# Spectral filter gated by a feed-forward net: the last residue chunk kept in SBUF, output rows requested half a tile sooner, another order at the second chunk's start

## The chip, the cores and the metric

The kernel runs on one core of a Trainium2 chip. The metric is the device time of one execution in microseconds; the time before is the median of three runs. The engines are named as in the profile: PE is TensorE, DVE is VectorE, ACT is ScalarE, POOL is GpSimd, SP is SyncE, whose queue issues most of the DMAs.

## The reference

```
xn  = layernorm(x)                                   # x: 1 x 2048 x 1024
s   = irfft2(rfft2(xn) * (w_r + 1j * w_i))           # over both axes
g   = silu(silu(xn @ w1) @ w2)                       # w1: 1024 x 3584, w2: 3584 x 1024
out = x + s * g
```

All is in float32.

## The kernel before

**Chunks and rows.** The 2048 rows of x are cut into 4 chunks (c) of 4 x 128 rows (p). In every large product the operands are split into a high and a low float16 half, and three passes are summed in PSUM: high by high, high by low and low by high.

**First stage** (0 to about 610 us): per chunk the layer norm, a transposed copy `xnT[c]` in both halves (`hi` and `lo` of `ln_gen` for chunks 0 and 1, DMA transposes in `turned` for chunks 2 and 3), and then `mm1(c, f)`: the product of one chunk with 128 columns of w1, 24 matmuls of 512 columns. A list `order` fixes in which order the pairs (c, f) run: chunk 0 with f = 0 to 3, chunk 1 with f = 0 to 3, and so on. Products are taken depth by depth, so that each needs both halves from the start; the pair (0, 0) alone takes the high-by-high pass first, then high by low, then low by high. `weights1` splits the columns of w1 just ahead of them (line 251 the high half on ACT, line 254 the low half on DVE). The hidden layer is written to DRAM as seven sums for seven products.

**FILL.** At two pairs (c, f) a piece of the spectral transform, `fa_mat` (24 matmuls of 128 columns into a PSUM buffer of the pool `pt`, tag `ft`, two buffers), is put ahead of `mm1`, with `fa_evac`, which copies it out with two ACT instructions (lines 775 and 776). The first is put at the pair (1, 0).

**Second stage**: seven products `(m, j)`, m from 0 to 6 and j from 0 to 7, each tile 42 matmuls of 512 columns in two halves k of 21, whose results are combined to the four blocks of `h @ w2`. Half way through each tile come `settle`, `load_parts` (loads of partial sums pl, line 527), `tick` (deferred stores) and `work` (a slot of background work); at the end of the tile `acc` registers what is to be done with the result, and the same calls follow. A result's evacuation runs half a tile later, its silu (line 615) at that tile's end, and half a tile after that `finish_out`: on DVE the product with the rows of s (line 608) and the sum with the rows of x (line 609), then the output store (line 611). Results become final in the products m = 4, 5 and 6 (`FINALS`). The rows that they need, fs from the residue s (kept in the DRAM tensors sd) and fx from x, are requested by `acc` through `rows_for` (line 548). The last tile (6, 7) is cut into pieces of 256, 128 and 128 columns.

**Background work**: beside both stages run generators for the spectral transform, one slot at a time. A planner with a clock of PE and one of DVE, advanced by fixed costs of each instruction that is written, decides how many slots are emitted between two products. The inverse transform `i_gen(c)` goes over the chunks in the order `IORDER` = 1, 3, 0, 2: it loads the chunk's coefficients (`zt`, one buffer of 16 KB a partition), copies the edge terms into them (line 1166 for an even chunk), multiplies (`mat`, line 1189 or 1181), combines, multiplies again (`mat2`, line 1271), and `bfly(p)` writes the residue's rows s of one block p (lines 1308 to 1315), which are then stored to sd (line 1326). Chunk 1 and 3 are done when m = 4 reaches the tiles that use them, chunk 0 and 2 later.

**Order on the queues.** The program is written in a fixed order, and each engine takes its instructions in that order; SP's DMAs wait in their turn for the buffers and the data that they need. `tile_of` hands out buffers of a tag, and stores that hold a buffer are written before their turn when it runs short.

Of the kernel before, what the change touches and what calls it, by code (L numbers as in the profile page):

```python
# [10 lines left out]
F32 = mybir.dt.float32  # L11
# [12 lines left out]
IORDER = (1, 3, 0, 2)  # L24
SUMMED = (4, 5)
TURNED = (2, 3)
FILL = ((1, 0), (3, 0))
EXTRA = (4, 5, 6, 7, 20, 22, 24)


# [97 lines left out]
def spectral_ffn(ctx, tc, x, w_r, w_i, w1, w2, ca, kc, ci, tw, pm, out):  # L128
    nc = tc.nc
# [45 lines left out]
    def tick():  # L175
        due = []
        for d in deferred:
            d[0] -= 1
            if d[0] <= 0:
                due.append(d)  # L180
        for d in due:
            deferred.remove(d)
            d[1]()
# [19 lines left out]
    def tile_of(pool, shape, dtype, name, tag, bufs):  # L203
        while len(held.get(tag, ())) >= bufs - 1:
            d = held[tag][0]
            deferred.remove(d)
            d[1]()
        return pool.tile(shape, dtype, name=name, tag=tag, bufs=bufs)
# [240 lines left out]
    def mm1(c, f):  # L449
        ps = pf.tile([128, 512], F32, name=f"pa{c}_{f}", tag="ff")  # L450
        w, xt = w1t[f], xnT[c]
        terms = [(d, wh, xh) for wh, xh in ((0, 0), (0, 1), (1, 0)) for d in range(8)]
        if c + f:
            terms.sort(key=lambda k: k[0])
        for n, (d, wh, xh) in enumerate(terms):
            nc.tensor.matmul(ps, w[:, wh, d], xt[:, xh, d], start=(n == 0), stop=(n == 23))  # L456
        if c == 3:
            used1.add(f)
        q, g = f // 2, c // 2

        def evac():
            if (q, g) not in h32:
                h32[q, g] = H["p"].tile([128, 4, 512], F32, name=f"h32_{q}_{g}", tag="h32", bufs=2)
            hq = h32[q, g]
            nc.scalar.activation(hq[:, 2 * (c % 2) + f % 2], ps, AF.Silu, scale=s1[:, f:f + 1])  # L465
            if c % 2 and f % 2:
                return hidden(q, g)

        return evac
# [37 lines left out]

        return second

    stile, queues, fins, sstore = {}, {}, {}, {}  # L510
    part, ht = {}, {}

    def load_h(m, j, k, queue=nc.scalar):
# [7 lines left out]
    rows = {}  # L521
    READS = ((), (), (), (), (1, 0), (), (2, 0))

    def load_parts(m, j):
        for k in READS[m]:
            t_ = tile_of(H["p"], [128, 512], F32, f"pl{m}_{j}_{k}", "pt", 6)
            nc.sync.dma_start(t_, pd[k, j])
            part[k, j] = t_
# [11 lines left out]
    def rows_for(c, p, h, pool, tags):  # L540

        hsl = slice(h * 512, (h + 1) * 512)
        if (c, p) in sstore:
            sstore.pop((c, p))()
        t_ = []
        for name, src, (tag, bufs) in (("fs", sd[c, p], tags[0]), ("fx", xs[4 * c + p], tags[1])):
            t_.append(tile_of(pool, [128, 512], F32, f"{name}{c}_{p}_{h}", tag, bufs))
            nc.sync.dma_start(t_[-1], src[:, hsl])
        return t_

    def acc(m, j, ps, cols=slice(0, 512)):
        tt = nc.vector.tensor_tensor
        g, p = j // 4, j % 4
        tags = (("kept", 8), ("kept", 8)) if m == 6 else (("fs", 3), ("fx", 2))
        for c, h in FINALS[m]:
            if (2 * g + c, p) in stile and (2 * g + c, p, h) not in rows:
                rows[2 * g + c, p, h] = rows_for(2 * g + c, p, h, H["p"], tags)

        def fresh(name):
            return tile_of(H["p"], [128, 512], F32, f"{name}_{j}", "pt", 6)  # L560

        def keep(k, t_):
            store("pt", 3, lambda: nc.sync.dma_start(pd[k, j], t_))

        def evac():
            if m == 0:
                kept[j] = H["p"].tile([128, 512], F32, name=f"kept{j}", tag="kept", bufs=8)
                nc.scalar.activation(kept[j], ps, AF.Copy)
            elif m == 1:
                t_ = fresh("c11")  # L570
                tt(t_, kept[j], ps, op=OP.subtract)
                keep(0, t_)
            elif m == 2:
                tt(kept[j], kept[j], ps, op=OP.add)
            elif m == 3:
                t_ = fresh("c21")
                nc.scalar.activation(t_, ps, AF.Copy)
                tt(kept[j], kept[j], ps, op=OP.subtract)
                keep(1, t_)
            elif m == 4:  # L580
                t_, u = part.pop((1, j)), part.pop((0, j))
                tt(t_, t_, ps, op=OP.add)
                tt(u, u, ps, op=OP.add)
                keep(0, u)
                return final(2 * g + 1, p, 0, t_)
            elif m == 5:
                t_ = fresh("c12")
                nc.scalar.activation(t_, ps, AF.Copy)
                tt(kept[j], kept[j], ps, op=OP.add)
                keep(2, t_)  # L590
                return final(2 * g + 1, p, 1, kept.pop(j))
            else:
                t_, u = part[2, j][:, cols], part[0, j][:, cols]
                tt(t_, t_, ps, op=OP.subtract)  # L594
                tt(u, u, ps, op=OP.add)
                a_, b_ = final(2 * g, p, 1, t_, cols), final(2 * g, p, 0, u, cols)

                def both():
                    x_, y_ = a_(), b_()
                    return (lambda: (x_ and x_(), y_ and y_(), None)[2]) if x_ or y_ else None  # L600

                return both

        return evac
# [534 lines left out]
    def load_i(c):  # L1139
        zt = C["p"].tile([128, 8192], F16, name=f"zt{c}", tag="zt", bufs=1)  # L1140
        if c % 2:
            src = zd[c].rearrange("(m e) q h (r x) -> r m e (q h) x", e=2, r=2)
            dst = zt.rearrange("m (e k x) -> m e k x", e=2, k=8)
            for r in range(2):
                for e in range(2):
                    nc.sync.dma_start(dst[64 * r:64 * r + 64, e], src[r, :, e])
        else:
            nc.sync.dma_start(zt.rearrange("m (q h x) -> m q h x", q=4, h=2), zd[c])
        k = C["p"].tile([128, 2064], F16, name=f"kk{c}", tag="kk", bufs=1)
        nc.sync.dma_start(k, ki[c])  # L1150
        C["z"][c], C["k"][c] = zt, k

    def i_gen(c):
        ip = C["p"]
        tt, stt = nc.vector.tensor_tensor, nc.vector.scalar_tensor_tensor
# [105 lines left out]
            stt(s_[:, 1], u, 2.0**-18, s_[:, 0], op0=OP.mult, op1=OP.subtract)  # L1261
            us[g] = s_

        psd = {}

        def mat2(p):
            ps = pt.tile([128, 4, 256], F32, name=f"id{c}_{p}", tag="ft")
# [8 lines left out]
        def bfly(p):  # L1276
# [14 lines left out]
            pc, qp, u, t_ = pa[:, 0, 0], pa[:, 0, 1], pa[:, 1, 0], pa[:, 1, 1]  # L1291
            pm_, qm, r, v = dm[:, 0, 0], dm[:, 0, 1], dm[:, 1, 0], dm[:, 1, 1]
            o12 = kf[:, 0:256].rearrange("s (n d) -> s n d", n=2)
            s_ = ip.tile([128, 8, 128], F32, name=f"s{c}_{p}", tag="s", bufs=2)
            sides = s_.rearrange("s a (h d) -> s (a h) d", h=2)

            def both(j):
# [17 lines left out]
            stt(both(3), pair(o12[:, 1]), -RH, pair(qp), op0=OP.mult, op1=OP.add)  # L1315
            sf = s_.rearrange("s a b -> s (a b)")
            stile[c, p] = True
            waiting = [h for h in range(2) if (c, p, h) in fins]
            for h in waiting:
                hsl = slice(h * 512, (h + 1) * 512)  # L1320
# [1 line left out]
                nc.sync.dma_start(o, gd[c, p, h])  # L1322
                nc.sync.dma_start(x_, xs[4 * c + p][:, hsl])
                finish_out("fs", c, p, h, o, sf[:, hsl], x_)
            if len(waiting) < 2:
                sstore[c, p] = lambda: nc.sync.dma_start(sd[c, p], sf)
                defer(1, lambda: (c, p) in sstore and sstore.pop((c, p))())

# [7 lines left out]
            yield 3.9 if 2 <= i <= 4 else 2  # L1336
        if c != IORDER[-1]:
            load_i(IORDER[IORDER.index(c) + 1])
        yield PAUSE
        for p in range(5):  # L1340
            if p < 4:
# [45 lines left out]
    with tc.manual_schedule():  # L1387
# [134 lines left out]
        for n, (m, j) in enumerate(seq):  # L1522
            if 0 < n < len(seq) - 2:
                for k in range(n == 1, 2):
                    load_h(*seq[n + 2], k, nc.scalar)
            if n == len(seq) - 1:
                load_parts(m, j)
                for b, cols in enumerate((slice(0, 256), slice(256, 384), slice(384, 512))):
                    ps = pf.tile([128, cols.stop - cols.start], F32, name=f"pb{m}_{j}_{b}", tag="ff")
                    for k in range(2):  # L1530
                        mm2(m, j, ps, k, cols)
                    for _ in range(4):
                        settle()
                        tick()
                    after(acc(m, j, ps, cols))
                break
            ps = pf.tile([128, 512], F32, name=f"pb{m}_{j}", tag="ff")
            for k in range(2):
                while ready2[0] < m * NP + 7 * k + 6:
                    slot(wq)  # L1540
                mm2(m, j, ps, k)
                if k == 0:
                    settle()
                    load_parts(m, j)
                    tick()
                    work()
            if j == 7:
                done2[0] = m + 1
            after(acc(m, j, ps))
            if m == 0:  # L1550
                slot(wq)
# [38 lines left out]
```

## Time and profile before

| what | value |
|---|---|
| median of three runs | 1242.93 us (1242.85 to 1243.19) |
| the profiled execution | 1243.2 us |
| its span, first to last instruction | 1241.3 us |
| PE busy | 1221.6 us, 98% |
| DVE busy | 999.3 us, 80% |
| ACT busy | 468.2 us, 38% |
| POOL busy | 116.0 us, 9% |
| DMA | 297.87 MB, mean 240 GB/s |

A busy PE is not PE at its peak, since matmuls are pipelined. Idle time of an engine that isn't the bottleneck costs nothing; what counts is where PE, or the stretch behind its last matmul, waits. A line of the timeline has start and duration in us, the engine, the line of the kernel, the operation, what is written from what, and in brackets the idle time ahead of it and what ended it.

### The profile page before, as it was taken

The page shows a single profiled execution, that of the slowest core. Times are in us where ns is not written, and L with a number is a line of the kernel's source. Part 1 is how long each engine was busy: PE and PEld are TensorE (multiplying, and loading weights), DVE is VectorE, ACT ScalarE, POOL GpSimd, SP SyncE. Part 2 cuts the span into 40 slices and gives each one's busy share as a digit, 9 for nine tenths or more (in the row PEclk, how much of TensorE's full clock was granted, in tenths as well). Part 3 has the DMA queues.
Part 4 walks back from the last instruction along what each step waited for, and adds up shares of the span by engine and source line. Part 5 has one row for each costly group of instructions (what it writes and reads, how often), then busy time and mean ns, then how long its engine had stood idle before and what let it go on. Part 6 is the DMA issues. An engine that isn't in the chain of part 4 may idle for free.

```text
span 1241.3 us, 19106 instructions
## 1 busy us (share of the span) xinstructions
PE 1221.6 (98%) x7033; PEld 625.4 (50%) x7033; DVE 999.3 (80%) x1974; ACT 468.2 (38%) x614; POOL 116.0 (9%) x241
## 2 busy tenths in 40 slices
PE   8999999999999999999999999999999999899997
PEld 5545445444544454445445555544545555455554
DVE  7687988899798898887969899794297588796886
ACT  4865344334554555435433222122132232242212
POOL 2230000001000000010001121114111110000000
PEclk9999999999999999999999999999999999999999
DMA  7487486646668897759899999997989989887797
GB/s 254 134 172 182 134 231 203 187 140 175 204 189 243 279 275 235 221 183 270 189 293 250 282 260 206 270 261 224 293 214 283 285 286 342 311 326 267 269 334 247
DMA packets 272831, 297.87 MB, mean 240 GB/s; under 512 B 40289, under 2 KB 199009, under 8 KB 272353
## 3 DMA queue, kind: packets, MB, share of 16 engines
q1 hardware_dynamic: 252720, 237.85, 66.1%
q10 hardware_dynamic: 15984, 51.45, 11.9%
q0 software_dynamic: 4032, 7.34, 3.4%
q8 instruction: 55, 0.90, 0.3%
q14 instruction: 40, 0.32, 0.1%
HBM read 188.05 MB, written 104.35 MB: 236 GB/s over the span
## 4 chain that ended last, share of the span: by engine, by line
PE 71%; DVE 13%; DMA 10%; issue 3%; ACT 2%; SPq 1%; POOL 0%; ACTq 0%; DVEq 0%; POOLq 0%
PE pa L456 45%; PE pb L536 7%; PE pb L535 7%; PE pb L534 7%; DVE Z L1039 2%; DMA fx<-in_A_x_dram 2%; PE id L1271 1%; DMA zd<-zq 1%; DMA wq<-in_A_w_i_dram 1%; DVE w L254 1%; DVE T L1004 1%; DMA pl<-pd 1%; DMA zt<-zd 1%; DMA ht<-hd_sum_d 1%; DVE zq L970 1%
## 5 line engine op out<-in xcount | busy, mean ns | idle before, releaser
L456 PE MATMUL pa<-xnT,w 128*128 128x512 f16 x2688 | 585.2, 379 | 1.1 <-ACT w L251 0.7
L456 PEld LDWEIGHTS <-w 128*128 128x128 f16 x2688 | 262.1, 98 | 311.7 <-DVE w L254 1.3
L534 PE MATMUL pb<-w,ht 128*128 128x512 f16 (+2 forms) x812 | 300.4, 372 | 0.0
L535 PE MATMUL pb<-w,ht 128*128 128x512 f16 (+2 forms) x812 | 300.4, 372 | 0.0
L536 PE MATMUL pb<-w,ht 128*128 128x512 f16 (+2 forms) x812 | 300.3, 372 | 0.0
L536 PEld LDWEIGHTS <-ht 128*128 128x128 f16 x812 | 79.4, 98 | 91.0
L534 PEld LDWEIGHTS <-ht 128*128 128x128 f16 x812 | 79.5, 98 | 86.9
L535 PEld LDWEIGHTS <-ht 128*128 128x128 f16 x812 | 79.5, 98 | 86.9
L465 ACT ACTIVATE h<-pa,s 128x512 f32<-128x512 f32 x112 | 75.6, 679 | 121.9 <-PE pa L456 109.8
L251 ACT ACTIVATE w<-jr,sc 128x512 f16<-128x512 f32 x98 | 68.2, 713 | 80.9 <-PE pb L536 25.4
L254 DVE SCALAR_TENSOR_TENSOR hoone<-h,hs,hoone 128x2048 f16<-128x2048 f32 x28 | 65.7, 2346 | 8.4 <-ACT hoone L251 8.4
L254 DVE SCALAR_TENSOR_TENSOR w<-jr,sc,w 128x512 f16<-128x512 f32 x98 | 71.1, 744 | 1.2 <-ACT w L251 1.2
L251 ACT ACTIVATE hoone<-h,hs 128x2048 f16<-128x2048 f32 x28 | 56.0, 1998 | 37.5 <-DVE h L499 24.6
L251 ACT ACTIVATE hosum<-hr,hs 128x1536 f16<-128x1536 f32 x28 | 44.1, 1574 | 64.8 <-DVE hr L495 31.2
L965 ACT ACTIVATE zq<-Z,zs 128x1024 f16<-128x1024 f32 x16 | 18.4, 1148 | 104.8 <-DVE Z L1039 57.8
L254 DVE SCALAR_TENSOR_TENSOR hosum<-hr,hs,hosum 128x1536 f16<-128x1536 f32 x28 | 50.7, 1812 | 3.4 <-ACT hosum L251 3.4
L494 DVE TENSOR_TENSOR hr<-h 128x1024 f32<-128x1024 f32 x28 | 34.2, 1222 | 23.9 <-ACT h L465 23.8
L251 ACT ACTIVATE w<-w1r,rs 128x1024 f16<-128x1024 f32 x28 | 32.0, 1144 | 47.0 <-DVE w L254 31.8
L274 DVE TENSOR_REDUCE m<-w1r 128x1 f32<-128x1024 f32 x28 | 33.8, 1211 | 16.5 <-DMA w1r<-in_B_w_dram 16.5
L615 ACT ACTIVATE pl<-pl,c 128x512 f32<-128x512 f32 (+2 forms) x28 | 17.4, 656 | 76.3 <-DVE pl L594 44.5
L938 PE MATMUL fx<-vq,kq 128*128 128x256 f16 x192 | 43.2, 272 | 0.0
L939 PE MATMUL fx<-vq,kq 128*128 128x128 f16 x192 | 42.0, 219 | 0.0
(210 smaller groups left out, 1524.5 us busy)
## 6 DMA issues: line engine op xcount, KB each, us to landing
w1r<-in_B_w_dram SPq DMA_DIRECT2D x28, 512.0 KB, 6.3
hd_sum<-hosum SPq DMA_DIRECT2D x56, 256.0 KB, 2.9
hd_one<-hoone SPq DMA_DIRECT2D x56, 256.0 KB, 3.6
hd_dif<-hoone SPq DMA_DIRECT2D x56, 256.0 KB, 3.2
w2m<-in_B_w_dram SPq DMA_DIRECT2D x28, 512.0 KB, 5.2
ht<-hd_dif ACTq DMA_DIRECT2D x32, 448.0 KB, 6.2
jr<-in_B_w_dram SPq DMA_DIRECT2D x56, 256.0 KB, 6.4
ht<-hd_sum ACTq DMA_DIRECT2D x32, 448.0 KB, 6.6
```

Of the source, the lines that this page charges most:

```text
L251: nc.scalar.activation(hi, raw, AF.Copy, scale=scale)
L254: nc.vector.scalar_tensor_tensor(lo, raw, scale, hi, op0=OP.mult, op1=OP.subtract)
L274: nc.vector.tensor_reduce(m1[:, i:i + 1], raw[i], axis=AX.XY, op=OP.max, apply_absolute_value=True)
L456: nc.tensor.matmul(ps, w[:, wh, d], xt[:, xh, d], start=(n == 0), stop=(n == 23))
L465: nc.scalar.activation(hq[:, 2 * (c % 2) + f % 2], ps, AF.Silu, scale=s1[:, f:f + 1])
L494: tt(sums[:, 0:2], hq[:, 0::2], hq[:, 1::2], op=OP.subtract)
L534: nc.tensor.matmul(ps, hh[:, 0], w[:, 0], start=first, stop=False)
L535: nc.tensor.matmul(ps, hh[:, 0], w[:, 1], start=False, stop=False)
L536: nc.tensor.matmul(ps, hh[:, 1], w[:, 0], start=False, stop=last)
L938: nc.tensor.matmul(o, k[:, c, kh, 1], v[:, c, vh], start=(n == 0), stop=False)
L939: nc.tensor.matmul(ps[:, c, 0], k[:, c, kh, 2], v[:, c, vh, 128:256], start=False, stop=False)
L1039: eng.tensor_tensor(Z[:, ns, pos], x0[:, :, ls], x1[:, :, ls], op=o_)
```

## The change

Three things are changed.

1. The first fill moves from the pair (1, 0) to the pair (1, 1), and `mm1(1, 0)` takes its high-by-high pass first, as (0, 0) does.
2. A function `ahead_rows`, taken out of `acc`, requests the rows for a tile's final results half way through that tile, right behind `load_parts`; in the last tile it is called ahead of the three pieces. `acc` still calls it for rows that weren't there yet.
3. The rows s of the chunk that is transformed last, chunk 2, are written into one tile of 4 blocks that takes the buffer of `zt`. They aren't stored to sd, and `rows_for` hands out views of that tile in place of loads.

```diff
-FILL = ((1, 0), (3, 0))
+FILL = ((1, 1), (3, 0))
...
     def mm1(c, f):
...
-        if c + f:
+        if f or c > 1:
             terms.sort(key=lambda k: k[0])
...
     def rows_for(c, p, h, pool, tags):
...
         for name, src, (tag, bufs) in (("fs", sd[c, p], tags[0]), ("fx", xs[4 * c + p], tags[1])):
+            if name == "fs" and (c, p) in resident:
+                t_.append(resident[c, p][:, hsl])
+                continue
             t_.append(tile_of(pool, [128, 512], F32, f"{name}{c}_{p}_{h}", tag, bufs))
             nc.sync.dma_start(t_[-1], src[:, hsl])
...
-    def acc(m, j, ps, cols=slice(0, 512)):
-        tt = nc.vector.tensor_tensor
+    def ahead_rows(m, j):
         g, p = j // 4, j % 4
         tags = (("kept", 8), ("kept", 8)) if m == 6 else (("fs", 3), ("fx", 2))
         for c, h in FINALS[m]:
             if (2 * g + c, p) in stile and (2 * g + c, p, h) not in rows:
                 rows[2 * g + c, p, h] = rows_for(2 * g + c, p, h, H["p"], tags)
+
+    def acc(m, j, ps, cols=slice(0, 512)):
+        tt = nc.vector.tensor_tensor
+        g, p = j // 4, j % 4
+        ahead_rows(m, j)
...
         def bfly(p):
...
-            s_ = ip.tile([128, 8, 128], F32, name=f"s{c}_{p}", tag="s", bufs=2)
+            if c == IORDER[-1]:
+                s_ = last_rows[0][:, p]
+            else:
+                s_ = ip.tile([128, 8, 128], F32, name=f"s{c}_{p}", tag="s", bufs=2)
...
             stile[c, p] = True
+            if c == IORDER[-1]:
+                resident[c, p] = sf
...
-            if len(waiting) < 2:
+            if len(waiting) < 2 and c != IORDER[-1]:
                 sstore[c, p] = lambda: nc.sync.dma_start(sd[c, p], sf)
...
         if c != IORDER[-1]:
             load_i(IORDER[IORDER.index(c) + 1])
+        else:
+            last_rows.append(ip.tile([128, 4, 8, 128], F32, name="rows", tag="zt", bufs=1))
...
             if n == len(seq) - 1:
                 load_parts(m, j)
+                ahead_rows(m, j)
...
                 if k == 0:
                     settle()
                     load_parts(m, j)
+                    ahead_rows(m, j)
                     tick()
                     work()
```

More of the change, by code (lines that the diff above doesn't have):

```diff
@@ L508, in hidden @@
         return second
-    stile, queues, fins, sstore = {}, {}, {}, {}
+    stile, queues, fins, sstore, resident = {}, {}, {}, {}, {}
     part, ht = {}, {}
@@ L1262, in split @@
             us[g] = s_
-        psd = {}
+        psd, last_rows = {}, []
         def mat2(p):
```

## The prediction

> **What bounds the kernel now.** I read the page first, then every wait of TensorE (PE) in the span, then the three places where those waits lie, engine by engine.
>
> ```profile
> span 1241.3 us, 19106 instructions
> ```
>
> ```profile
> PE iu L1189 <- DVE zt L1166: 2.8, 1, 2.8
> ...
> PE pa L456 <- DVE w L254: 0.4, 1, 0.4
> ```
>
> The first fence is the page's head, the second the view of waits for PE alone (us in total, times, longest). TensorE waits in very few places, and the change touches three of them: the start, where the second chunk's first product is prepared; the 2.8 us before the third chunk's inverse transform; and the stretch after PE's last matmul, which no wait of PE shows. The windows view below has one short and one long stretch (length, then PE, PEld, DVE, ACT, POOL busy with counts, granted clock, DMA share, GB/s).
>
> ```profile
> 49.36:63.10 13.74, 13.74 (x67) 6.39 (x66) 7.33 (x17) 13.61 (x10) 4.31 (x12) 1.00 0.75 144
> 70.00:840.00 770.00, 770.00 (x4230) 382.74 (x4229) 666.53 (x1248) 322.56 (x381) 63.29 (x115) 1.00 0.79 221
> ```
>
> From 70 to 840 us PE is busy for 770.00 of 770 us: what is lost or won before 70 us is kept to the end, one for one. From 49.36 to 63.10 us ScalarE (ACT) is busy for 13.61 of 13.74 us: anything put into its queue there delays everything behind it. These two rows decide the first part.
>
> **Part 1: the fill and the order of the second chunk's first product.** The timelines of PE, ACT and VectorE (DVE), columns start, duration, instruction, and in brackets the idle time before it and who ended it:
>
> ```profile
> 41.97 1.95 PE L702 MATMUL tp<-ident,x 128*128 128x128 f32 x16
> 45.40 0.22 PE L766 MATMUL fa<-cas,xnT 128*128 128x128 f16 x1 [1.47 <-DVE xnT L710]
> ...
> 46.73 10.52 PE L456 MATMUL pa<-xnT,w 128*128 128x512 f16 x48
> ...
> 68.61 1.69 PE L456 MATMUL pa<-xnT,w 128*128 128x512 f16 x7 [0.42 <-DVE w L254]
> ```
>
> ```profile
> 43.06 1.94 ACT L706 ACTIVATE xnT<-tp 128x1024 f16<-128x1024 f32 x2 [3.09 <-PE tp L702]
> ...
> 46.94 0.61 ACT L775 ACTIVATE L<-fa 128x520 f32<-128x520 f32 x1 [1.36 <-PE fa L768]
> 47.44 0.59 ACT L776 ACTIVATE L<-fa 128x504 f32<-128x504 f32 x1
> 47.91 0.69 ACT L465 ACTIVATE h<-pa,s 128x512 f32<-128x512 f32 x1
> ```
>
> ```profile
> 44.12 2.36 DVE L710 TENSOR_TENSOR xnT<-tp,xnT 128x1024 f16<-128x1024 f32 x2 [2.12 <-ACT xnT L706]
> ...
> 63.26 1.23 DVE L494 TENSOR_TENSOR hr<-h 128x1024 f32<-128x1024 f32 x1 [4.95 <-ACT h L465]
> ...
> 67.27 1.28 DVE L254 SCALAR_TENSOR_TENSOR w<-w1r,rs,w 128x1024 f16<-128x1024 f32 x1
> ```
>
> Before, PE waits 1.47 us for a PSUM buffer, runs the 24 fill matmuls (45.40 to 46.73, so 1.33 us) and then product (1,0) from 46.73. After, (1,0) comes first and its eight high-by-high matmuls need only the high halves, which ACT finishes at 43.06 + 1.94 = 45.00. A matmul takes 10.52/48 = 0.219 us here, so those eight run to about 46.8; the low halves are there at 44.12 + 2.36 = 46.48, so the next pass doesn't wait. PE then runs (1,0) for 24 x 0.219 = 5.25 us and the fill: it gets through about 0.35 us sooner (45.05 against 45.40).
>
> But the two copies of the fill's result (L775, L776) move too. Before, they stand in ACT's queue at 46.94 and take 47.91 - 46.94 = 0.97 us, in a stretch where ACT waits anyway. After, they are written into the program ahead of (1,1) and so behind the normalisation steps that the first background slot after (1,0) emits: inside the stretch from 49.36 to 63.10 that has no room. That slot is emitted either way: the planner's clock of PE is one fill lower there, which isn't enough to hold it back by its constants. So everything that ACT does behind them comes 0.97 us later, with the evacuation h for which DVE waited 4.95 us at 63.26, and behind this in DVE's order the low half of the next weights (L254, done at 67.27 + 1.28 = 68.55), for which PE waited 0.42 us at 68.61. I therefore expect PE at 69.58 instead of 68.61, its wait growing to 0.42 + 0.35 + 0.97 = 1.74 us: **+0.97 us**. If ACT's delay is hidden after all, this part gives -0.35; these are its ends. I take the upper one, since the row of ACT's stretch leaves 0.13 us free.
>
> **Part 2: rows asked for half a tile sooner (fifth to seventh product).** Three timelines' rows around the 2.8 us wait: SP's queue, DVE, and how long the residue's stores (L1326) take to land (min/median/max).
>
> ```profile
> 1050.36 0.44 SPq L548 DMA_DIRECT2D fs<-sd  x1
> 1050.85 0.42 SPq L548 DMA_DIRECT2D fx<-in_A_x_dram  x1
> ...
> 1053.34 0.90 SPq L527 DMA_DIRECT2D pl<-pd  x2
> ```
>
> ```profile
> 1056.84 0.75 DVE L608 SCALAR_TENSOR_TENSOR pl<-fs,s_sc,pl 128x512 f32<-128x512 f32 x1 [1.78 <-DMA fs<-sd]
> 1059.27 0.69 DVE L609 TENSOR_TENSOR pl<-pl,fx 128x512 f32<-128x512 f32 x1 [1.67 <-DMA fx<-in_A_x_dram]
> 1060.65 0.69 DVE L582 TENSOR_TENSOR pl<-pl,pb 128x512 f32<-128x512 f32 x1 [0.69 <-DMA pl<-pd]
> ```
>
> ```profile
> DMA to landing us min/median/max: 3.5/5.6/9.6
> ```
>
> PE's 2.8 us end with the copy at L1166, which stands in DVE's queue right behind these. DVE waits 1.78 us for fs, 1.67 for fx and 0.69 for the partial sums pl. Asked for half a tile sooner, fs and fx are there, so 3.45 us of waiting go; but what is late next is pl, which is asked for at 1053.34 whatever fs does and was waited for last. Only what pl itself moves up counts. The two requests in front of it (0.44 + 0.42 us of SP's time) have then been issued a round earlier, so I take 0.86, say **-0.9 us**. The ends: -2.8 if pl comes so much sooner that the whole wait goes; and a loss, because the moved request sits behind the store it reads. For the chunk whose residue is being made at that time, a row's load must wait for its own store, and before it stood behind four other transfers, now it stands ahead of them: the store of the partial sum, the store of the output, the weights jr and the next pl all queue on SP behind that wait. A store lands after 5.6 us in the median; the half tile gained is about as long, so what is held up is of the order of 0 to 3 us: +3.0 is my upper end. On the issue of a load behind the store that it reads, the Trainium skill's page "DMA: Bandwidth & Descriptors", section "Two DMAs through the same engine are not ordered", says that the same queue gives no order and that the issuing engine has to wait for the first transfer's semaphore. By that page's fixed 2.0 us plus bytes over 436 GB/s, a 512 KB store would cost 3.2 us, my estimate; the row's median of 5.6 is longer and is what I go by.
>
> In the seventh product the second tile's four loads share eight buffers with a result of the sixth product whose output store is written behind them. One of the loads has to wait for that store; behind it on SP stand only a partial sum's store and the next tile's loads, needed more than a tile later: nothing.
>
> **Part 3: the last chunk's rows stay in SBUF.** Four stores of 512 KB and eight loads of 256 KB go. The room is that of the chunk's transform input, which PE has read before the first row is written; no wait is added. Until the last tile this all lies beside PE. Then:
>
> ```profile
> 1220.82 0.95 SPq L527 DMA_DIRECT2D pl<-pd  x2
> ```
>
> ```profile
> 1229.40 4.72 DMA fx<-in_A_x_dram
> ```
>
> ```profile
> 1232.23 0.48 DVE L608 SCALAR_TENSOR_TENSOR pl<-fs,s_sc,pl 128x256 f32<-128x256 f32 x1 [3.69 <-DMA fs<-sd]
> 1232.90 0.43 DVE L609 TENSOR_TENSOR pl<-pl,fx 128x256 f32<-128x256 f32 x1 [0.19 <-DMA fx<-in_A_x_dram]
> 1233.57 0.48 DVE L608 SCALAR_TENSOR_TENSOR pl<-fs,s_sc,pl 128x256 f32<-128x256 f32 x1 [0.24 <-DMA fs<-sd]
> 1234.21 0.42 DVE L609 TENSOR_TENSOR pl<-pl,fx 128x256 f32<-128x256 f32 x1 [0.16 <-DMA fx<-in_A_x_dram]
> ...
> 1236.48 0.28 DVE L594 TENSOR_TENSOR pl<-pl,pb 128x128 f32<-128x128 f32 x1
> ```
>
> ```profile
> 1232.22 0.22 PE L536 MATMUL pb<-w,ht 128*128 128x128 f16 x1
> ```
>
> PE's last matmul ends at 1232.22 + 0.22 = 1232.44, but DVE takes up its result only at 1236.48, since the first of the last tile's three pieces waited 3.69 + 0.19 + 0.24 + 0.16 = 4.28 us for rows (the piece of the chain of waits: a load issued at 1229.40, 4.72 us). After, fs is no transfer, and the two fx loads are issued right behind pl, at about 1221.8 and 1222.3: with 4.72 us each they land by 1227, before DVE wants them at 1232.23 - 3.69 = 1228.54. Without the 4.28 us DVE would reach the last piece at 1232.20, so PE's end is what is late next: about 1232.5. From there to the span's end nothing changes (1241.3 - 1236.48 = 4.82 us). That is **-3.98 us**; a few tenths of activation in front of the first piece are covered by PE's end. The ends are -4.04 and, if the loads don't get ahead, about -1.0 (below).
>
> **The sum**, against the profiled execution's own 1243.2 us (span 1241.3 and 1.9 around it): 0.97 - 0.9 - 3.98 = -3.91, so 1239.3; the median of the three runs, 1242.93, lies 0.27 lower, which gives 1239.0 us.
>
> **The rivals.**
> - *The start gains.* ACT's delay is swallowed and part 1 gives -0.35: 1.32 us less, 1237.7. Against it: the row of ACT's stretch and the 4.95 us for which DVE waits on it.
> - *The middle doesn't gain.* The moved requests hold up about as much as they bring: part 2 between 0 and +3.0, so 1239.9 to 1242.9. For it: pl is the last wait, and it isn't moved.
> - *The tail's loads don't get ahead*, so the change doesn't do there what it says: SP keeps the two fx behind the waiting output stores, and only the two fs issues go, moving the last load from 1229.40 to about 1228.4. Tail -1.0 instead of -3.98: 1242.0. Against it: the call stands in the program directly behind pl's.
> - *Slower: the store-to-load wait on SP.* In tiles 4 to 7 of the fifth product a request goes out right behind a store that takes the longest landing of the row, 9.6 us, and pl, queued behind it, comes 9.6 us later; PE's wait before the third chunk's transform grows from 2.8 to 12.4 us: 1243.2 + 0.97 + 9.6 - 3.98 - 0.27 = 1249.5. It turns the sign beyond the resolution once the hold-up exceeds 2.5 + 3.98 - 0.97 = 5.5 us. For it: TensorE's longest wait hangs on exactly this queue. Against: most landings are near 5.6 us, and the request is made half a tile before its use. The Trainium skill, "TensorE: Matmul & The Clock Gate", section "HAM oscillation — how this bites in real kernels", adds that PE gaps above about 3.4 us bring the clock down; by it this case would cost a little more, and no wait so long stands inside this trace.
>
> **How the numbers follow.** A measurement of this kernel tells 0.2%, about 2.5 us, from no change: faster means below 1240.4, slower above 1245.4. The forecast gets 0.45 and the start's gain 0.15, both faster. The middle gets 0.22, of which 0.08 lies below 1240.4 and 0.14 within. The tail's rival gets 0.10, within; the slower one 0.08. That is faster 0.68, same 0.24, slower 0.08. The range goes from 1236.5 (the start's gain with somewhat more in the middle) to 1243.0 (the middle's upper end); it leaves out the slower case and the rare sum of all gains (-0.35 - 2.8 - 4.04, so 1235.7).
>
> **What would show it.** In the profile after: PE's wait for the fill gone and its wait on the weights' low half at about 1.7 us near 69 us; a wait of about 1.9 us instead of 2.8 before the third chunk's transform, with DVE waiting on pl and hardly on fs or fx; no wait of L608 in the last tile, its last piece taken up within 0.2 us of PE's last matmul, and some 4.8 us from there to the end. I am wrong in part 1 if ACT's copies of the fill delay no h, in part 2 if SP's loads behind the stores grow PE's wait, and in part 3 if the last piece still starts 2 us or more after PE ends.

## The result: slower by two parts in a thousand, and the profile after

| | before | after |
|---|---|---|
| median of 22 executions each (lowest to highest) | 1242.51 us (1239.79 to 1246.35) | 1244.91 us (1240.88 to 1249.37) |
| ratio after / before, 95% interval | | 1.0022 [1.0012, 1.0032] |
| profiled execution, its span | 1243.2 us, 1241.3 us | 1245.52 us, 1243.7 us |
| TensorE's last matmul ends, and from there to the span's end | 1232.44, 8.90 us | 1239.04, 4.66 us |

In the two profiles the change takes 4.2 us off the tail and puts 6.5 us into the middle. Lines stand further down in the kernel after (L548 of before is L551, L608 is L615, L1166 is L1173, L1326 is L1338). The longest wait of PE in the kernel after (us in total, times, longest):

```profile
PE iu L1196 <- DVE zt L1173: 7.5, 1, 7.5
```

Before, this wait was 2.8 us: it is the middle. I go through the three places, start, middle and tail, in order.

**The start came out as written.** PE, ACT and DVE in the kernel after:

```profile
44.94 5.34 PE L456 MATMUL pa<-xnT,w 128*128 128x512 f16 x24 [1.13 <-ACT xnT L713]
...
69.47 3.84 PE L456 MATMUL pa<-xnT,w 128*128 128x512 f16 x17 [1.74 <-DVE w L254]
```

```profile
55.60 0.59 ACT L782 ACTIVATE L<-fa 128x520 f32<-128x520 f32 x1
```

```profile
64.12 1.23 DVE L494 TENSOR_TENSOR hr<-h 128x1024 f32<-128x1024 f32 x1 [6.26 <-ACT h L465]
```

The product starts at 44.94 without waiting for the low halves, the two copies now stand from 55.60 on, inside ACT's full stretch, DVE gets its h 0.86 us later (64.12 against 63.26), and PE waits 1.74 us where it waited 0.42.

**The middle went the other way.** PE, then DVE in the kernel after:

```profile
1066.97 6.91 PE L1196 MATMUL iu<-kk,zt 128*128 128x129 f16 x72 [7.51 <-DVE zt L1173]
```

```profile
1058.91 0.75 DVE L615 SCALAR_TENSOR_TENSOR pl<-fs,s_sc,pl 128x512 f32<-128x512 f32 x1
...
1063.92 0.69 DVE L589 TENSOR_TENSOR pl<-pl,pb 128x512 f32<-128x512 f32 x1 [3.54 <-DMA pl<-pd]
1066.11 0.69 DVE L590 TENSOR_TENSOR pl<-pl,pb 128x512 f32<-128x512 f32 x1 [1.50 <-DMA pl<-pd]
```

DVE waits no more for fs or fx, and pl is the last wait, both as expected. But pl is asked for at 1059.73 instead of 1053.34. SP's queue in the kernel after, and then the same place before:

```profile
1028.24 0.32 SPq L1338 DMA_DIRECT2D sd<-s  x1
1039.84 0.32 SPq L551 DMA_DIRECT2D fs<-sd  x1
...
1040.69 0.46 SPq L570 DMA_DIRECT2D pd<-pl  x1
...
1059.73 2.47 SPq L527 DMA_DIRECT2D pl<-pd  x2
```

```profile
1033.35 0.32 SPq L563 DMA_DIRECT2D pd<-pl  x1
1033.77 0.38 SPq L1326 DMA_DIRECT2D sd<-s  x1
...
1038.66 0.32 SPq L548 DMA_DIRECT2D fs<-sd  x1
```

After, SP issues the store of the first of these residue tiles at 1028.24, and its next instruction, the load of the same rows, goes out at 1039.84: for 11.3 us SP issues nothing. Before, the store went out 5.5 us later (1033.77) and the load 1.2 us sooner (1038.66). So asking half a tile sooner moved the store up but not the load, and the store of the partial sum (pd), which stood ahead of both at 1033.35, came behind them, at 1040.69. The view of SP's waits splits the 11.3 us between two landings (us in total, times, longest): 5.1 us for the transform input zt, then 6.1 for the store.

```profile
SPq L551 <- DMA sd<-s: 7.4, 2, 6.1
...
SPq L551 <- DMA zt<-zd: 5.1, 1, 5.1
```

The chain of waits shows what slides behind (start, us, what):

```profile
1028.24 11.58 DMA sd<-s
...
1042.23 8.62 DMA sd<-s
...
1052.81 9.05 DMA out_dram<-pl
1061.88 4.21 DMA pl<-pd
```

The store took 11.58 us to land, the second 8.62, and the output store that went out late behind them holds the buffer into which the second pl is loaded. The landing of all residue stores was 3.5/5.6/9.6 us (min/median/max) before; after:

```profile
DMA to landing us min/median/max: 4.7/8.2/12.8
```

A second loss stands in PE's row: the 72 matmuls take 6.91 us. The windows view, first after, then before (length, then PE, PEld, DVE, ACT, POOL busy with counts, granted clock, DMA share, GB/s):

```profile
1062.00:1067.00 5.00, 0.03 (x1) 0.03 (x2) 1.49 (x3) 1.33 (x2) 0.00 (x0) 0.53 0.95 267
1067.00:1075.00 8.00, 8.00 (x78) 7.30 (x79) 4.13 (x10) 1.15 (x4) 0.00 (x0) 0.65 0.82 290
```

```profile
1062.00:1067.00 5.00, 4.20 (x71) 4.03 (x71) 2.62 (x5) 1.89 (x5) 0.00 (x0) 1.00 1.03 381
```

The granted clock is 0.53 in the second part of the long gap and 0.65 behind it. Before, with a gap of 2.8 us, it stays at 1.00, and PE's next product starts 5.00 us after the first of the same matmuls (1067.11 - 1062.11, a wait of 0.70 included) instead of 6.74 (1073.71 - 1066.97).

**The tail came out as written.** SP and DVE in the kernel after:

```profile
1226.85 0.95 SPq L527 DMA_DIRECT2D pl<-pd  x2
1227.85 0.91 SPq L551 DMA_DIRECT2D fx<-in_A_x_dram  x2
```

```profile
1235.39 0.48 DVE L615 SCALAR_TENSOR_TENSOR pl<-rows,s_sc,pl 128x256 f32<-128x256 f32 x1 [0.25 <-ACT pl L622]
...
1239.08 0.29 DVE L601 TENSOR_TENSOR pl<-pl,pb 128x128 f32<-128x128 f32 x1
```

No DMA stands in a bracket of these pieces any more, and DVE takes up the last one at 1239.08, 0.04 us after PE's end.

**The sum by places.** Each number is how much later than in the profile of before the same matmul of the products starts (the same place in PE's order), at about 73 us, at 1020 us (the middle not yet begun) and behind the third chunk's first transform product (1067.11 us before). The last two columns are from PE's end to the span's end, and the span.

| kernel (experiments below) | 73 us | 1020 us | 1067 us | middle: 1067 less 1020 | tail | span |
|---|---|---|---|---|---|---|
| before | 0 | 0 | 0 | 0 | 8.90 | 1241.34 |
| after | +0.86 | +0.15 | +6.60 | +6.45 | 4.66 | 1243.70 |
| e1_no_ahead_4_7 | +0.85 | +3.22 | +2.23 | -0.99 | 4.66 | 1239.34 |
| e2_other_rows | +0.88 | +0.73 | +0.44 | -0.29 | 4.66 | 1237.54 |
| e3_only_4_7 | -0.14 | +3.38 | +6.10 | +2.72 | 9.66 | 1248.20 |
| e4_tail_only | -0.33 | -1.03 | -2.11 | -1.08 | 4.65 | 1234.98 |
| e5_filled_gap | +0.70 | -0.01 | +4.06 | +4.07 | 4.65 | 1241.15 |
| e6_start_only | +0.82 | +0.80 | -0.29 | -1.09 | 9.25 | 1241.40 |
| e7_calm_tiles | -0.28 | +3.07 | +2.38 | -0.69 | 4.65 | 1239.46 |
| e8_fx_early | +1.27 | +5.13 | +4.60 | -0.53 | 4.66 | 1241.70 |
| e9_store_act | +1.29 | +1.45 | +6.31 | +4.86 | 4.65 | 1243.40 |
| e10_resident_only | -0.12 | +4.56 | +3.10 | -1.46 | 7.63 | 1243.17 |
| e11_ask_only | -0.05 | -0.72 | -2.25 | -1.53 | 6.29 | 1236.48 |
| e12_both | -0.26 | -0.97 | -2.78 | -1.81 | 4.65 | 1234.32 |

For after: 0.15 + 6.45 - 4.24 = +2.36, the difference of the spans. From 1067 us to PE's end no kernel moves by more than 0.01 us. The column at 1020 us needs care: e3, e4, e10, e11 and e12 issue up to there what before issues, and yet they stand between -1.03 and +4.56 us there (why, stands in the last section). So one profile's span says little at this size; the columns "middle" and "tail" and the ratios over many executions do. The other kernels without early requests in tiles 4 to 7 of the fifth product (e8's for x aside) have a middle of -0.7 to -1.8, so the profile of before was itself on the long side there by some 1 us. A tail that nothing changes took 8.90, 9.25 and 9.66 us (before, e6, e3).

### The profile page after: what moved, and what is told of

Same layout as the page of the kernel before. It is cut to its first block, busy times and chain, and to the rows that moved or that the text cites. A ratio compares the mean times of both kernels' runs of the same rounds, so it can differ in the third digit from the quotient of the medians.

```text
span 1243.7 us, 19101 instructions
## 1 busy us (share of the span) xinstructions
PE 1222.9 (98%) x7033; PEld 627.7 (50%) x7033; DVE 999.3 (80%) x1974; ACT 467.6 (38%) x614; POOL 115.8 (9%) x241
## 4 chain that ended last, share of the span: by engine, by line
PE 88%; DMA 5%; DVE 4%; ACT 2%; issue 1%; SPq 0%; POOL 0%; ACTq 0%; DVEq 0%; POOLq 0%
PE pa L456 45%; PE pb L536 12%; PE pb L534 12%; PE pb L535 12%; PE fx L945 2%; DMA sd<-s 2%; PE id L1278 1%; DMA out_dram<-pl 1%; PE iu L1196 1%; PE fx L947 1%; PE fx L946 1%; DMA jr<-in_B_w_dram 1%; ACT xp L700 1%; PE fa L773 1%; PE iu L1188 1%
```

## The experiments

Each kernel ran beside the kernel before on the same chip, and its ratio is to those executions; three chips were used (e1 to e4, e5 to e8, e9 to e12), so medians in us are compared within one of these groups only. Each median is of 12 executions (e3: 6), and each profile is of one.

Theory: part 2 costs, because in tiles 4 to 7 of the fifth product a load now stands directly behind the store of the rows it reads, SP waits there until the store has landed, and pl is queued behind it. Rivals: the start costs more than its 1 us; any early request costs through fuller DMA engines; the resident rows cost something.

### Take the early requests out of those four tiles

```
                     load_parts(m, j)
-                    ahead_rows(m, j)
+                    if m != 4 or j < 4:
+                        ahead_rows(m, j)
```

> The kernel after, but in tiles 4 to 7 of the fifth product (m = 4) the rows are requested at the tile's end as before. Theory (the hold): there SP stands at a load that must wait for the store it reads, and pl is asked for late; without it PE's wait before the third chunk's transform (7.5 us after, 2.8 before) falls to 4 us or less, the granted clock stays at 1.00 in that stretch, and the time is 3 to 5 us below the kernel before (tail -4.2, start +0.15). Rival (elsewhere): the early requests of the other tiles or the missing stores move the queue; then the wait stays at 6 us or more and the time is 1 to 3 us above the kernel before.

Measured: median 1240.26 us, ratio to before 0.9981 [0.9966, 0.9995].

```profile
PE iu L1196 <- DVE zt L1173: 1.8, 1, 1.8
```

```profile
1062.00:1070.00 8.00, 5.48 (x79) 4.46 (x78) 4.85 (x11) 2.26 (x5) 0.00 (x0) 1.00 1.04 385
```

With four requests moved back, the wait is 1.8 us, the clock 1.00, and the kernel is faster than before. The middle is 7.44 us shorter than in the kernel after: its loss is in these four tiles. The time fell by less than expected, 2.0 us below before (1242.28 here) instead of 3 to 5; in the trace 3.22 us arose ahead of 1020 us.

### Keep the early requests, but read rows that are already stored

The load of fs takes rows of the second chunk, stored long ago, in place of the fourth's (so these rows of the output are wrong).

```
+        src_c = 1 if c == 3 and h == 0 else c
-        for name, src, (tag, bufs) in (("fs", sd[c, p], tags[0]), ...
+        for name, src, (tag, bufs) in (("fs", sd[src_c, p], tags[0]), ...
```

> The kernel after with the same order, count and size of transfers, but in tiles 4 to 7 of the fifth product fs is read from the residue of the second chunk, stored long before, in place of the fourth chunk's just stored (so these output rows carry the wrong residue). Theory (the hold): no load waits for a store, PE's wait falls to 3 us or less and the time is 3 to 5 us below the kernel before. Rival (order and bandwidth): two transfers of 256 KB stand ahead of what DVE needs whether they wait or not; then PE's wait stays at 6 to 8 us and the time is 1 to 3 us above the kernel before.

Measured: median 1242.03 us, ratio 0.999 [0.9976, 1.0004]. SP's queue, then PE's wait:

```profile
1028.63 0.32 SPq L1339 DMA_DIRECT2D sd<-s  x1
1034.86 0.32 SPq L552 DMA_DIRECT2D fs<-sd  x1
```

```profile
PE iu L1197 <- DVE zt L1174: 2.5, 1, 2.5
```

Same instructions, same order, same bytes; only the load no longer reads what the store writes. SP waits 5.9 us (for the landing of the transform input, not of the store) instead of 11.3, PE 2.5 us instead of 7.5. So it is the wait for the store's landing, not the traffic; of the 11.3 us, 5.9 would have passed without it. The expected time, 3 to 5 us below before, was missed: the interval of the ratio reaches from -3.0 to +0.5 us. Against the kernel after, the ratios differ by 0.0032, 4.0 us, which is less than the trace's 6.7 (6.45 + 0.29).

### Only those four tiles' requests, on the kernel before

```
+                    if m == 4 and j >= 4:
+                        ahead_rows(m, j)
```

> The kernel before with the early request in tiles 4 to 7 of the fifth product alone. Theory (the hold): this alone makes PE wait 6 to 8 us, the clock falls behind the wait, and with no gain in the tail the time is 5 to 7 us above the kernel before. Rival (order and bandwidth): two transfers of some 0.65 us each, 0 to 1.5 us above the kernel before.

Measured: median 1250.26 us, ratio 1.0057 [1.0039, 1.0076], so +7.1 us. PE's wait and the windows:

```profile
PE iu L1193 <- DVE zt L1170: 4.3, 1, 4.3
```

```profile
1062.00:1070.00 8.00, 3.71 (x34) 3.12 (x32) 1.49 (x3) 1.48 (x3) 0.00 (x0) 0.79 0.95 298
```

Four requests alone make the kernel clearly slower, and the price agrees with the difference of the ratios of after (1.0022) and the tail alone (0.9964), 0.0058. But in its one profile PE's wait is only 4.3 us, where 6 to 8 were expected, and the middle +2.72; 3.38 of its span arose ahead of the first of these requests and 0.76 in the tail. How much of the 7.1 us in six executions is the four requests' own is therefore open. A gap of 4.3 us too is followed by a clock below 1.00.

### Only the tail part

The kernel after with the start undone and without `ahead_rows` in mid tile (the last tile's call stays).

> The kernel before with the last chunk's rows in SBUF and the early request in the last tile alone (start and all other tiles as before). Theory: the tail's -4.2 us are all here and the middle is untouched: PE's wait 2 to 4 us, time 3.5 to 5 us below the kernel before. Rival (the tail needs the early requests of the tiles ahead of it): a gain of 1 to 3 us.

Measured: median 1237.39 us (1235.32 to 1242.6), ratio 0.9964 [0.9948, 0.998]; tail 4.65 us. This version beats both kernels. It ran again on another chip, beside its two halves, as e12_both below.

### Fill the gap in front of the transform

In the kernel after, 50 matmuls on idle data go ahead of the transform's first product, into the same PSUM tile.

```
             psu[g] = ps
+            if c == 0 and g == 0:
+                for _ in range(50):
+                    nc.tensor.matmul(ps[:, 0:256], idle[:, 0:128], idle, start=True, stop=True)
```

> The changed kernel, with 50 idle matmuls of 256 columns (about 5.4 us) put on TensorE ahead of the third chunk's first transform product, into a gap of 7.5 us there. Theory: the granted clock of 0.52 to 0.80 after that gap is made by the gap itself. Then the 72 matmuls after it take about 5.2 us as before instead of 6.9, the clock in 1062 to 1075 us stays at 0.95 or more, and the time is 1.7 us below the changed kernel's: about 1243.2, ratio to before 1.0006. Rival: the clock falls there for another reason (the power state of that moment, as it does in 845 to 855 us in some runs): the 72 matmuls still take 6.5 us or more and the time stays at 1244.9. In both the wait for the last row and its transfer stay as long as they were.

Measured: median 1244.74 us, ratio 1.0014 [1.0001, 1.0027]. PE, then the windows:

```profile
1059.13 5.62 PE L1184 MATMUL iu<-ones 128*128 128x256 f16 x50
1066.17 2.92 PE L1201 MATMUL iu<-kk,zt 128*128 128x129 f16 x48 [1.42 <-DVE zt L1173]
```

```profile
1062.00:1067.00 5.00, 3.58 (x41) 3.06 (x39) 1.49 (x3) 1.33 (x2) 0.00 (x0) 1.00 0.89 251
1067.00:1075.00 8.00, 7.30 (x79) 5.05 (x77) 5.31 (x12) 2.46 (x5) 0.00 (x0) 1.00 0.79 299
```

The data still comes late (1066.17), but the clock stays at 1.00 and from there to the next product it takes 5.00 us (1071.17 - 1066.17) instead of 6.74. So the gap makes the clock fall, and that costs 1.74 us of the 6.45. The times can't tell: the median lies near the rival's 1244.9 us, but before ran 0.65 us longer here than in the first table, and the ratio's interval holds the theory's 1.0006 as well as 1.0022.

### Only the start

> The kernel before with only the first part of the change: the filler moved to the second column block and the second chunk's first product sorted high-by-high pass first. Theory: TensorE stands 0.8 to 1.0 us later at 73 us, and 0.1 to 0.9 us later from 850 us on, since a wait for the edge product there takes part of it back; 1242.5 to 1243.4, ratio 1.0001 to 1.0008. Rival: the start is worth 3 us at the end (the difference of the kernel without requests in tiles 4 to 7 and the one with only the tail part, 1240.3 against 1237.4): 1245.

Measured: median 1242.88 us, ratio 0.9998 [0.9985, 1.0011]. PE:

```profile
69.43 2.76 PE L456 MATMUL pa<-xnT,w 128*128 128x512 f16 x12 [1.74 <-DVE w L254]
```

The wait is there to the hundredth and PE is 0.82 us late at 73 us, but over 12 executions nothing can be measured: the interval reaches from -1.9 to +1.4 us. The rival of 3 us is out.

### Early requests everywhere but in the four tiles, start as before

> The kernel with only the tail part, and rows asked for half a tile sooner in all tiles but 4 to 7 of the fifth product, that is, wherever no store of the same rows is pending. Theory: without a store to wait for, the early requests change nothing that TensorE waits for: 1236.9 to 1237.9, within 0.5 us of the kernel with only the tail part (1237.4), TensorE's wait for the third chunk's transform input at 1.5 to 2.8 us. Rival: early requests cost wherever they stand, through the DMA queues: 1239 to 1240.

Measured: median 1240.74 us, ratio 0.9973 [0.9958, 0.9988], against 0.9964 [0.9948, 0.998] with the tail alone on another chip. PE's wait is 2.1 us, the middle -0.69, and 3.07 us of its span came up ahead of 1020 us. The median missed the expected 1236.9 to 1237.9. On this chip before ran 0.9 us longer too; with that taken off, it lies in the rival's range (1239 to 1240), and the two ratios can't be told apart. What speaks against the rival is the trace, where neither the wait nor the middle shows a cost. A gain of these requests isn't seen either.

### Ask early for x alone in the four tiles

```
+                    else:
+                        early[c, p, 0] = tile_of(H["p"], [128, 512], F32, f"fx{c}_{p}_0", "fx", 2)
+                        nc.sync.dma_start(early[c, p, 0], xs[4 * c + p][:, 0:512])
```

> The changed kernel, but in tiles 4 to 7 of the fifth product only the rows of x are asked for in mid tile; the rows of the residue, and with them their store, come at the end of the tile as before. Theory: it is the wait of the residue rows' load for their store's landing that holds the queue: without it pl of tile 4 is asked for by 1054 us and TensorE waits 1.7 to 2.8 us; about 1240.3, as without any early request there. Rival: any 256 KB more in that stretch pushes pl back: the wait is 4 to 6 us and the time 1242 to 1243.5.

Measured: median 1242.06 us, ratio 0.9985 [0.997, 1.0].

```profile
PE iu L1201 <- DVE zt L1178: 2.3, 1, 2.3
```

In the trace an early load in the same place does no harm if it reads nothing that is being stored: the wait is within the theory's 1.7 to 2.8, not the rival's 4 to 6, and the middle is -0.53. The ratio is near that of e1 (0.9981), but the median lies in the rival's range (1242 to 1243.5). pl was asked for at 1058.30 in its trace, but PE itself stood 5.13 us later there, so the 1054 of the expectation isn't a fair mark.

### Issue the store on another queue

```
-                sstore[c, p] = lambda: nc.sync.dma_start(sd[c, p], sf)
+                sstore[c, p] = lambda: nc.scalar.dma_start(sd[c, p], sf)
```

> The changed kernel, with the stores of the residue's rows issued on ScalarE's DMA queue instead of SyncE's. Theory: the store took 11.6 us to land because it stood behind a 2 MB load in its own queue; on the other queue it lands within 6 us, SyncE is held at most 5 us, pl of tile 4 is asked for by 1056 us and TensorE waits 2 to 4 us there; about 1241, ratio 0.998 to 1.0. Rival: it lands late because all queues share the same 16 DMA engines: it still takes 9 us or more, the wait stays at 6 us or more, and the time at 1.001 to 1.003.

Measured: median 1245.59 us, ratio 1.0009 [0.9993, 1.0025]. The chain of waits and PE's wait:

```profile
1027.24 11.61 DMA sd<-s
```

```profile
PE iu L1196 <- DVE zt L1173: 6.0, 1, 6.0
```

My theory here was wrong. The store doesn't land late because it stands behind the 2 MB transform input in SP's queue: on ScalarE's queue it takes 11.61 us, as on SP's (11.58). The view of DMAs counts all queues against the same 16 engines, and those are full: 1026 to 1042 us of the kernel after in 40 slices, busy tenths and GB/s:

```profile
DMA  9989799999989697999999999999974209576999
GB/s 384 503 321 530 291 506 387 454 442 378 408 336 555 253 518 324 405 302 294 284 286 291 261 354 389 400 430 420 410 312 184 102 20 87 102 128 113 224 347 319
```

They work through a backlog until about 1038 us, and move little around 1039.84, when the held load at last goes out: SP has issued nothing in the meantime. That the backlog, and not a place in a queue, makes the store late is my reading: ScalarE's queue too had two loads ahead of the store, issued at 1020.15 and 1020.96.

### The two halves of the tail, and both

Rows kept in SBUF without the early request in the last tile; the early request without the rows kept; both (the same kernel as e4).

> The kernel before, with the last chunk's rows kept in SBUF, and the last tile's rows of x asked for where they were before, after the tile's first piece. Theory: two loads instead of four are issued about 1228 us; they land 1.3 us sooner (two landings of 0.65 us fewer), so the end comes 0.7 to 1.5 us sooner: tail 7.4 to 8.2 us after TensorE's end instead of 8.9, ratio 0.9988 to 0.9994. Rival: keeping the rows is what shortens the tail: 4.7 us after TensorE's end, ratio 0.9965.

> The kernel before, with only the last tile's rows asked for ahead of that tile's products, all four loads, and no row kept in SBUF. Theory: asked for about 6 us sooner, all four land by 1229 us, ahead of the first piece, and the tail falls to 4.7 to 5.2 us after TensorE's end, all of the part's gain: ratio 0.996 to 0.997. Rival: four loads in place of two still end last: tail 6 to 7.5 us, ratio 0.998 to 0.999.

> The kernel with only the tail part (rows kept and asked for early, nothing else of the change), on the same chip as the two halves of it. Theory: tail 4.7 us after TensorE's end, ratio 0.9964 as in its other run, within 0.001. If the gain of its other run (4.9 us in the medians against 4.2 in the trace) was partly luck, 0.9966 to 0.9975.

Measured: ratios 0.9986 [0.9972, 1.0], 0.9966 [0.9948, 0.9984] and 0.9963 [0.9949, 0.9978]; medians 1241.21, 1238.36 and 1237.77 us. Tails 7.63, 6.29 and 4.65 us. DVE on the last tile's first piece, rows kept only, then asked early only:

```profile
1235.42 0.42 DVE L616 TENSOR_TENSOR pl<-pl,fx 128x256 f32<-128x256 f32 x1 [3.05 <-DMA fx<-in_A_x_dram]
```

```profile
1226.80 0.48 DVE L612 SCALAR_TENSOR_TENSOR pl<-fs,s_sc,pl 128x256 f32<-128x256 f32 x1 [0.51 <-DMA fs<-sd]
1228.05 0.42 DVE L613 TENSOR_TENSOR pl<-pl,fx 128x256 f32<-128x256 f32 x1 [0.77 <-DMA fx<-in_A_x_dram]
1228.67 0.49 DVE L612 SCALAR_TENSOR_TENSOR pl<-fs,s_sc,pl 128x256 f32<-128x256 f32 x1 [0.19 <-DMA fs<-sd]
1229.33 0.42 DVE L613 TENSOR_TENSOR pl<-pl,fx 128x256 f32<-128x256 f32 x1 [0.18 <-DMA fx<-in_A_x_dram]
```

Keeping the rows alone takes 1.27 us off the tail, as worked out from two landings fewer. Asking early alone takes 2.61; the four loads still end last, by 0.51 + 0.77 + 0.19 + 0.18 = 1.65 us, which is the 1.64 that is missing. Here the rival's tail (6 to 7.5 us) was right and my theory's was not, while the ratio came out in the theory's range (0.996 to 0.997). Neither half does it alone: the request gets the loads out in time, and the rows kept make them two instead of four. The ratios order the three in the same way, but their intervals don't part the last two.

## Why the prediction was wrong, point by point

**The step that failed is part 2**, "say **-0.9 us**", with an upper end of +3.0. What the runs put in its place is +6.45 us in the trace, and 4.0 to 7.1 us by the ratios (e2 and e1 against after, e3 against before). The wrong term is the hold-up behind the store: the forecast put pl 0.86 us sooner, and it was asked for 6.4 us later. The mechanism was on the page twice: in part 2, where SP's later transfers "queue on SP behind that wait", and as the slower rival. I took the wrong side with two mistakes in its size. The landing was taken at the median of 5.6 us, a value of all sixteen stores over 264 us; these stores go out while a 2 MB load is still moving, and the first took 11.58, longer than the longest row of before (9.6). And I set the half tile gained against that landing; but asking for the rows also issues the store, 5.5 us sooner and into the full engines (1028.24 instead of 1033.77, where it took 4.8 us to land), so the load behind it went out 1.2 us later than before. Nothing of the half tile was gained, and the stores that pl waits for came behind the hold.

**The slower rival** had 0.08. Its place was right (tiles 4 to 7 of the fifth product, pl behind it, PE's wait before the third chunk's transform); its price was not: pl was asked for 6.4 us later, not 9.6, and PE's wait grew to 7.5 us, not 12.4. The 6.45 us are 4.71 of waiting (7.51 less 2.81, to the rounding) and 1.74 of lower clock, which the rival's 1249.5 did not count. The Trainium skill, "TensorE: Matmul & The Clock Gate", section "HAM oscillation — how this bites in real kernels", gives idle gaps of more than about 3.4 us as what brings the clock down. This place agrees: gaps of 2.8 us (before) and less left it at 1.00, gaps of 4.3 (e3), 6.0 (e9) and 7.5 us were followed by a lower clock, and filling the gap kept 1.00 (e5). Another place, in the last section, isn't covered by it. The prediction named that rule, and gave it no chance and no price.

**By the other page** named in the prediction, "DMA: Bandwidth & Descriptors" of the Trainium skill, section "Anatomy of one DMA — SWDGE (gpsimd) path", whose fit is for one DMA on GpSimd's path, a store of this size would take 3.2 us by my estimate. The measured 11.58 and 8.62 differ, with the engines full.

**Right in part 2:** DVE's waits for fs and fx went, and pl is the wait that ends last.

**The rival that the middle doesn't gain** (0.22) pointed the right way, but ended at +3.0.

**Part 1** was right in mechanism and size: +0.97 worked out, +0.86 (after) and +0.82 (e6) measured at 73 us. That the wait is 1.74 us to the hundredth is luck: PE got there 0.46 us sooner, not 0.35, and ACT's copies delayed h by 0.86, not 0.97. That it "is kept to the end, one for one" was shown only from 70 to 840 us; there PE is busy for 770.00 of 770 us after the change too:

```profile
70.00:840.00 770.00, 770.00 (x4231) 382.86 (x4230) 668.22 (x1250) 323.08 (x382) 63.39 (x116) 1.00 0.79 221
```

At 1020 us it is +0.15 in one profile and +0.80 in the other, and stretches that the change doesn't touch differ there by more.

**Part 3** was right: -3.98 worked out, 8.90 - 4.66 = -4.24 measured, the last piece 0.04 us after PE's end. That is 0.2 beyond its end of -4.04, since from the last piece to the span's end 4.62 us passed (1243.70 - 1239.08) where 4.82 were worked out. Alone it is a ratio of 0.9964, some 4.5 us. That the tail's loads don't get ahead (0.10) didn't come about: they go out directly behind pl.

**The chances** were set from a median that stood for a place it wasn't measured in. With 11.6 us in place of 5.6, less the half tile ("about as long" as 5.6), the text's own sum gives a hold-up of 6 us, and its turning point of 5.5 is passed.

## What to carry to other kernels

A load moved ahead of its use isn't free when it reads what was just stored: on an in-order queue it stands there until the store has landed, and all that is queued behind it is late, urgent or not. So look up, for each request that is moved, which store it would then stand directly behind, and price that store's landing by what the DMA engines are doing at that moment, not by a median. A wait in front of TensorE can cost more than its length: here 7.5 us of it brought the granted clock down and cost 1.74 us more. And an edit with three parts deserves three runs: here one part earned some 4 us and another spent 4 to 7.

## What the runs showed that I had not expected

- A 512 KB store took 11.58 us on SP's queue and 11.61 on ScalarE's at the same place: there, another queue brought nothing.
- While SP waited for that landing the DMA engines moved little (20 to 128 GB/s from 1038.4 to 1040.8 us, after 250 to 555 up to 1038): the wait costs transfers, not only order.
- Kernels that issue the same instructions up to 1020 us stand there up to 5.6 us apart (-1.03 to +4.56), and nearly all of it arises within 12 us around 845, where the small edge product of the transform waits for GpSimd. PE's timeline there with the rows kept only (e10, +4.56), and PE's windows (length, PE busy with counts, granted clock, DMA share, GB/s):

```profile
844.49 0.40 PE L1076 MATMUL eps<-edge,perm 128*128 128x24 f32 x2 [0.87 <-POOL edge L1069]
...
845.39 0.39 PE L1078 MATMUL eps<-edge,perm 128*128 128x8 f32 x2 [0.21 <-POOL edge L1072]
```

```profile
844.00:846.00 2.00, 1.30 (x9) 0.99 0.00 0
846.00:848.00 2.00, 2.00 (x11) 0.50 0.00 0
...
850.00:852.00 2.00, 2.00 (x6) 0.50 0.86 272
852.00:854.00 2.00, 2.00 (x9) 0.80 1.00 371
```

PE waits 1.1 us in all between matmuls of 8 and 24 columns, and then runs at half clock for 6 us, which with the part at 0.80 costs 3.4 us. In before, where 0.30 us are idle there, and in e4, where none is, the clock stays at 1.00. All fourteen traces agree: the five in which PE is idle for 0.66 to 1.24 us around there (e1, e3, e7, e8, e10) show a granted clock of 0.50 to 0.56 in a window of 2 us behind it; the nine with 0.30 us or less show 1.00. So a lower clock followed idle times far below 3 us too; that the small matmuls between them make the difference is a reading, no run tried it. Why GpSimd's part comes in time in one execution and late in another I did not find out.
